# Places of VectorE sums and scalings, and paired final stores, in a fused attention and gated feed-forward kernel

## The chip, the cores and the metric

The kernel runs on one core of a Trainium2 chip. The metric is the device time of one execution in microseconds (us); for several executions the median is given. TensorE (PE) multiplies matrices into PSUM banks, VectorE (DVE) and ScalarE (ACT) work element by element, GpSimd (POOL) broadcasts rows, and SyncE (SP) issues the stores. Each engine takes its instructions in the order of the program and waits for the others by semaphores.

## The reference

Linear attention over 8 batches with 8 heads, 1024 tokens and 64 columns a head, then a feed-forward layer with a gate over the 8192 tokens:

```python
k_proj = np.einsum('ks,bhsd->bhkd', E, k)              # 64 rows instead of 1024
v_proj = np.einsum('ks,bhsd->bhkd', F, v)
attn = softmax(scale * q @ k_proj.T)                   # over the 64 rows
x = (attn @ v_proj) as 8192 tokens x 512
gate = 1 / (1 + exp(-(x @ w_gate)))                    # 512 x 1536
out = (gate * (x @ w_val)) @ w_out                     # 1536 x 512, float32
```

Inputs and output are float32; the kernel multiplies in bf16 and accumulates in float32.

## The kernel before, in words

**Tiles.** The tokens of a batch are worked in two blocks (`blk`) of 512. The attention of a batch leaves `xT`, 512 columns on four tiles of 128 partitions, for both its blocks. For a block, `x @ w_gate` is done whole (`g_step`, four matmuls of 512 columns), and `x @ w_val` and the product with `w_out` as Strassen-like products: seven half-size products in place of eight, for which VectorE first forms sums and differences of the operands. `xs_sums` (L1426) forms those of `x`, `s_sums` (L1228) those of the hidden values `hT`; `s_sums(blk, n, ms)` makes sum number n for the rows `ms`, where `A` = (0, 4) and `Z` = (4, 6) are two thirds and one third of them. Sum 1 writes S1, sum 2 S2 (from S1), sum 3 A21 in its place, sum 4 A12 in its place (from S2).

**Order.** The order on every engine is written out by hand. For the batches b = 1 to 7 a loop makes six units u, each a third of a block, with nine slots j: the pieces `p1`, `p26`, `p57`, `p4` of the value product (L1464, L1483 are their VectorE work: `hidden` and `v_add`), `g_step`s between them, and in slot 0 of the next unit the piece `p3` of the unit before. `on(u, j, fn)` puts other work behind slot j of unit u, in the order in which it was registered. `o0` = 2b - 1 and `o1` = 2b are the blocks whose product with `w_out` falls into this batch: `first_products` at (2, 0) and (5, 0), `last_products` at (2, 2) and (5, 2). `first_products(blk, hooks)` calls its hooks at fixed points; hook -1 lies between the product A12 x B21 and `add_snap(0, ...)`, which clears that product's bank, hook 0 behind `s_sums(blk, 4, ...)`, and hook 1 at the end.

**Attention in the background.** While batch b's feed-forward work runs, `attention(b + 1)` is laid between. At (3, 0) `outputs3` ends with eight small transfers (`gather`, L904) and 16 broadcasts on GpSimd (`spread`, L917), which give each of eight tiles its reciprocal denominators; `mul(r, g)` (L949) then scales that tile of `xu` into `xT`. There are eight scalings a batch. The last batch has no attention to prepare. Batch 0 has an order of its own, `todo` with `put(i, fn)`: there `bc2(R)` spreads the denominators of the second half by matmuls into two PSUM banks, and `scale` (L688) writes `xT` from them.

**Waits.** `Plan.add` notes what an instruction reads and writes, and waits are made of it. A matmul that starts a new product in a PSUM bank waits for whoever read that bank last, so `v_add`, `add_snap` and the gate (L1150) hold up TensorE if they are late:

```python
def p26():
    a = held_v["a"]
    held_v["c"] = c = FF.take()
    v_product(blk, q, c, "A12", "B21", start=True, stop=True)
    v_add(0, c)
    ...
def p57():
    a, c = held_v["a"], held_v["c"]
    v_product(blk, q, c, "S1", "T1", start=True)
```

**The end.** `final_products` (from L1330 on) does the last block's product with `w_out`, with VectorE's `plus` (L1347) and `add_snap` (L1280), and stores each quarter when it is there: eight stores of 128 rows of 1 KB from SP (L1340). The stores of the other blocks (L1325) have rows of 2 KB.

Of the kernel before, what the change touches and what calls it, by code (L numbers as in the profile page):

```python
# [118 lines left out]
def bass_linformer_attn__then__ffn_glu_sigmoid_kernel(  # L119
# [11 lines left out]
    B = q.shape[0]  # L131
# [6 lines left out]
    with contextlib.ExitStack() as es:  # L138
# [71 lines left out]
        ost = sbuf("ost", [P, 4, DM], FP32)  # L210
# [358 lines left out]
        def half_unit(hf, ring):  # L569
# [86 lines left out]
            def bc(R):  # L656
                bks = [ring.next(), ring.next()]
                for c in range(4):
                    for g in range(2):
                        n = 2 * R + g  # L660
                        nn = slice(32 * n, 32 * n + 32)
                        mm(
                            bks[g],
                            bank[bks[g]][:, c * P : (c + 1) * P],
                            (bsel8 if hf else bsel8f)[nn, c, :, :].rearrange("p h d -> p (h d)"),
                            (rhl if hf else rden)[nn, 0:P],
                            ["bsel8", ("rhl", R)] if hf else ["bsel8f", ("rden", 0, R)],
                            tp=(32 * n, 0),
                        )
                if hf:  # L670
                    for g in range(2):
                        scale(R, g, bank[bks[g]], xu[:, 2 * R + g, :], [("xu", 2 * R + g)], bks[g])

                def keep(g):
                    act(
                        xu[:, 2 * R + g, :],
                        bank[bks[g]][:, :],
                        [],
                        [("xu", 2 * R + g)],
                        b=bks[g],  # L680
                    )

                return keep
# [646 lines left out]
        def final_products(blk):  # L1330

            a, b, c, e0 = [AA.take() for _ in range(4)]
            e1 = FF.take()

            def store(tt, col, sem):
                t = 2 * (2 * (blk % 2) + tt % 2) + tt // 2
                cc = slice(256 * col, 256 * col + 256)
                add(
                    "SP",
                    lambda e: e.dma_start(out_v[blk // 2, t][:, cc], ost[:, tt, cc]),  # L1340
                    r=[("ost", tt, col)],
                    dma=sem,
                )

            def plus(o, keys, n, bk, jj):
                dve(
                    lambda e: e.scalar_tensor_tensor(  # L1347
                        o, bank[bk][:, jj], 0.5, snap[n][:, jj], ALU.mult, ALU.add
                    ),
                    [("snap", n)],  # L1350
                    keys,
                    b=bk,
                )

            product(blk, a, "A11", "B11", True)
            keep_snap(0, a)
            product(blk, c, "S1", "T1", True, True)
            product(blk, a, "S2", "T2")
            keep_snap(1, a)
            plus(snap[1], [("snap", 1)], 1, c, slice(0, 512))  # L1360
            product(blk, b, "A12", "B21", True, True)
            s_sums(blk, 4, (0, 6))
            add_snap(0, b, 0, 0)
            product(blk, a, "A21", "T3")
            keep_snap(2, a)
            add_snap(2, c, 1, 1)
            product(blk, e0, "A12", "B22", True, True, (0,))
            plus(ost[:, 0, 256:512], [("ost", 0, 1)], 1, e0, slice(0, 256))
            product(blk, a, "A22", "T4", stop=True)
            o, keys = quarter(1, 0)  # L1370
            act(o, bank[a][:, :].rearrange("p (j c) -> p j c", j=2), [], keys, b=a, scale=0.5)
            product(blk, e1, "A12", "B22", True, True, (1,))
            plus(ost[:, 1, 256:512], [("ost", 1, 1)], 1, e1, slice(256, 512))
            for tt, col in ((0, 0), (1, 0), (2, 1), (3, 1), (0, 1), (2, 0), (3, 0)):
                store(tt, col, f"out{tt}")
            store(1, 1, "outlast")

# [244 lines left out]
        put(5, lambda: (sc2(0), sc2(1)))  # L1624
        put(5, second_loads)
        put(7, lambda: (den2(), xo2(0), xo2(1)))
        put(9, lambda: (bc2(0), bc2(1)))
        for i, fn in zip((12, 14, 15, 16, 17, 18, 19, 19, 20, 21, 22), attention(1)):
            put(i, fn)
        put(16, lambda: (load_k(2), load_v(2), load_q(2)))  # L1630
# [27 lines left out]
        for b in range(1, B):  # L1658
            todo, at = [], {}
            for u in range(6):  # L1660
                K = 6 * b + u
                p1, p26, p57, p4, p3 = v_pieces(K)
                todo += [
                    last_piece,
                    p1,
                    lambda K=K: g_step(K, 1),
                    p26,
                    lambda K=K: g_step(K, 2),
                    p57,
                    lambda K=K: g_step(K, 3),  # L1670
                    p4,
                    (lambda K=K: g_step(K + 1, 0)) if K + 1 < 6 * B else (lambda: None),
                ]
                last_piece = p3

            def on(u, j, fn):
                put(9 * u + j, fn)

            def h_sums(blk, ms, *ns):
                return lambda: [s_sums(blk, n, ms) for n in ns]  # L1680

            def x_sums(blk, *ns):
                return lambda: [xs_sums(blk, n) for n in ns]

            A, Z = (0, 4), (4, 6)
            o0, o1 = 2 * b - 1, 2 * b
            if b == 1:
                first = {1: lambda: (vt_sums(1), vt_sums(4), x_sums(2, 1, 2, 3, 4)())}
                on(0, 0, lambda: first_products(o0, first))
                on(0, 2, lambda: last_products(o0))  # L1690
                on(0, 4, x_sums(3, 1, 2, 3, 4))
                on(2, 0, h_sums(o1, A, 1))
                on(2, 4, h_sums(o1, A, 2, 3))
            else:
                on(0, 4, h_sums(o0, A, 1, 2))
                on(1, 0, h_sums(o0, A, 3))
                on(1, 0, h_sums(o0, Z, 1))
                on(1, 4, h_sums(o0, Z, 2, 3))
                first = {
                    0: x_sums(o1 + 1, 1, 2, 3, 4),  # L1700
                    1: h_sums(o1, A, 1, 2, 3),
                }
                on(2, 0, lambda: first_products(o0, first))
                on(2, 2, lambda: last_products(o0))
            if b + 1 < B:
                n = attention(b + 1)
                late, keep_kv, mul = n["late"], n["keep_kv"], n["mul"]
                ks = 1 if b == 1 else 0
                for u, name in ((ks, "scores"), (ks + 1, "mixed")):
                    on(u, 0, n[name])  # L1710
                    on(u, 1, lambda: late("A0", 0))
                    on(u, 3, lambda: late("A0", 1))
                    on(u, 6, lambda: (late("A1", 0), late("A1", 1)))
                on(3, 0, n["outputs"])
                on(3, 0 if b + 2 < B else 4, h_sums(o1, Z, 1, 2, 3))
                on(3, 1, lambda: late("A0", 0))
                on(3, 3, lambda: late("A0", 1))
                on(3, 6, lambda: keep_kv(0))
                on(4, 1, lambda: keep_kv(1))
                on(4, 3, lambda: keep_kv(2))  # L1720

                on(4, 4, lambda: (mul(0, 0), mul(0, 1)))
                last = {
                    -1: lambda: mul(1, 0),
                    0: lambda: (mul(1, 1), mul(2, 0), mul(2, 1)),
                    1: lambda: (mul(3, 0), mul(3, 1)),
                }
                on(5, 0, lambda: first_products(o1, last))
                on(5, 4, x_sums(o1 + 2, 1, 2))
                on(5, 7, x_sums(o1 + 2, 3, 4))  # L1730
            else:
                on(3, 0, h_sums(o1, Z, 1, 2, 3))
                last = {1: h_sums(o1 + 1, A, 1, 2, 3)}
                on(5, 0, lambda: first_products(o1, last))
                on(5, 7, h_sums(o1 + 1, Z, 1, 2, 3))
            on(5, 2, lambda: last_products(o1))
            if b + 2 < B:
                kpd_ = [("kpD", R) for R in range(2)] if b == 1 else []
                load_at = (1, 4) if b == 1 else (0, 2)
                on(*load_at, lambda: (load_k(b + 2, kpd_), load_v(b + 2), load_q(b + 2)))  # L1740
                on(3, 4, transpose_q)
            for i, slot in enumerate(todo):
                slot()
                for fn in at.pop(i, ()):
                    fn()
            assert not at
# [31 lines left out]
```

## Time and profile before

| | |
|---|---|
| Median of 4 runs | 534.01 us (533.27 to 534.75) |
| Profiled execution: time, span | 533.24 us, 531.4 us |
| TensorE busy | 519.8 us, 98% of the span |
| VectorE busy | 407.4 us, 77% |
| ScalarE busy | 302.7 us, 57% |
| GpSimd busy | 133.5 us, 25% |
| Granted TensorE clock | 1.0 |

The span goes from the first to the last instruction of the profiled execution; the time of the same execution is 1.8 us longer. In the lists of groups and in the timeline, a line names start and busy time in us, then the engine, the line of the code, the operation, the tiles it writes and reads, their shapes, and how many instructions are merged; a bracket gives the idle time of the engine before it and what ended it. Many lines carry the number of a helper (L264 is every matmul, L268 every ACT instruction), so the tiles tell them apart: `wG` is the gate product, `wV` and `vT` the value product, `wO` and `wT` the product with `w_out`. In the waits, an engine stands left and what it waited for right, with the sum in us, the number of times and the longest. PEld is TensorE's loading of weights, which can run ahead of the matmuls.

### The profile page before, as it was taken

To read this page: it belongs to the slowest core of one execution; us is meant where nothing else is said; L and a number is where in the kernel's file an instruction comes from. 1 tells how busy PE (TensorE), PEld (TensorE's weight loads), DVE (VectorE), ACT (ScalarE), POOL (GpSimd) and SP (SyncE) were. 2 spreads that over 40 slices of the span, in tenths; PEclk is the share of its full clock that TensorE was granted. 3 is DMA by queue.
4 is the path that set the end of the run, shared out by engine and by line. 5 is a ranking of instruction groups with operands and counts; after the bars stand their busy time and mean duration, and the time that the engine had idled before them with its cause. 6 is when DMAs were issued, how large, how long until landed. Compare 5 with 4: busy or idle time off the path is not lost.

```text
span 531.4 us, 10382 instructions
## 1 busy us (share of the span) xinstructions
PE 519.8 (98%) x4137; PEld 347.4 (65%) x4137; DVE 407.4 (77%) x662; ACT 302.7 (57%) x544; POOL 133.5 (25%) x148
## 2 busy tenths in 40 slices
PE   5999999999999999999999999999999999999997
PEld 4544446656857667585766768576675867767676
DVE  4645495888987788877988789878888689887755
ACT  2554823687385564946567473755748464544541
POOL 9310200106700085002920048000740009200000
PEclk9999999999999999999999999999999999999999
DMA  9999999794293255911689233952520020202022
GB/s 171 200 199 203 161 203 214 151 177 87 35 228 63 80 92 85 230 42 47 88 165 153 80 60 36 220 96 80 92 80 1 1 83 2 81 0 80 1 81 79
DMA packets 77200, 56.18 MB, mean 106 GB/s; under 512 B 34848, under 2 KB 69344, under 8 KB 77152
## 3 DMA queue, kind: packets, MB, share of 16 engines
q0 software_dynamic: 33984, 29.89, 36.3%
q1 hardware_dynamic: 43168, 25.63, 19.8%
q8 instruction: 32, 0.52, 0.4%
q14 instruction: 16, 0.13, 0.1%
HBM read 60.29 MB, written 16.78 MB: 145 GB/s over the span
## 4 chain that ended last, share of the span: by engine, by line
PE 93%; DVE 3%; DMA 1%; issue 1%; POOL 1%; ACT 0%; SPq 0%; POOLq 0%; DVEq 0%
PE pF L264 60%; PE pA L264 32%; POOL KVs L917 1%; DMA EF<-in_F_dram 1%; DVE xT L949 1%; DVE rden L841 1%; DVE vsnap L1483 1%; DVE hT L1150 0%; DMA eT<-rden 0%; DVE rden L639 0%; DVE hS L1228 0%; DVE xT L688 0%; DVE ost L1280 0%; ACT vsnap L268 0%; ACT qT L268 0%
## 5 line engine op out<-in xcount | busy, mean ns | idle before, releaser
L264 PE MATMUL pF<-xT,wG 128*128 128x512 bf16 x768 | 197.9, 379 | 0.3
L917 POOL PARTITION_BROADCAST KVs<-eT x96 | 96.9, 1035 | 244.5 <-PE pF L264 191.7
L268 ACT ACTIVATE sig<-pF 128x512 f32<-128x512 f32 x192 | 115.6, 602 | 52.9 <-PE pF L264 50.9
L1483 DVE TENSOR_TENSOR vsnap<-pF,vsnap 128x512 f32<-128x512 f32 x126 | 86.8, 689 | 37.7 <-PE pF L264 28.0
L264 PEld LDWEIGHTS pF<-xT,wG 128*128 128x128 bf16 x768 | 73.7, 98 | 57.0 <-issue 1.7
L268 ACT ACTIVATE vsnap<-pF 128x512 f32<-128x512 f32 x126 | 75.3, 598 | 45.8 <-PE pF L264 43.1
L1464 DVE SCALAR_TENSOR_TENSOR hT<-sig,vsnap 128x512 bf16<-128x512 f32 x126 | 87.1, 691 | 6.2 <-ACT vsnap L268 0.5
L264 PE MATMUL pF<-xT,wV 128*128 128x256 bf16 (+1 forms) x432 | 76.1, 297 | 0.3 <-DVE hT L1150 0.3
L264 PE MATMUL pA<-wO,hT 128*128 128x256 bf16 x534 | 63.4, 273 | 0.0
L264 PEld LDWEIGHTS pF<-xT,wV 128*128 128x128 bf16 x432 | 40.6, 98 | 28.4 <-issue 5.3
L264 PEld LDWEIGHTS pA<-wO,hT 128*128 128x128 bf16 x534 | 52.2, 98 | 6.3
L264 PE MATMUL pF<-xS,wV 128*128 128x256 bf16 x336 | 50.5, 273 | 1.5 <-DVE vsnap L1483 1.4
L264 PE MATMUL pF<-xS,vT 128*128 128x256 bf16 x336 | 50.4, 273 | 0.0
L949 DVE TENSOR_TENSOR xT<-xu,KVs 128x512 bf16<-128x512 f32 x48 | 47.5, 1030 | 2.2 <-POOL KVs L917 1.7
L264 PEld LDWEIGHTS pF<-xS,wV 128*128 128x128 bf16 x336 | 32.0, 98 | 25.7 <-DVE vsnap L1483 6.6
L268 ACT ACTIVATE EF<-pA 128x512 f32<-128x512 f32 x30 | 17.9, 597 | 48.9 <-PE pA L264 48.9
L264 PE MATMUL pA<-wT,hT 128*128 128x256 bf16 x360 | 44.2, 273 | 0.0
L264 PE MATMUL pA<-wT,hS 128*128 128x256 bf16 x360 | 41.7, 273 | 0.0
L264 PEld LDWEIGHTS pA<-wT,hT 128*128 128x128 bf16 x360 | 35.1, 98 | 7.3 <-ACT snap L268 0.3
L264 PEld LDWEIGHTS pA<-wT,hS 128*128 128x128 bf16 x360 | 35.1, 98 | 4.2
L1280 DVE SCALAR_TENSOR_TENSOR ost<-pA,EF 128x512 f32<-128x512 f32 x29 | 20.0, 688 | 20.4 <-PE pA L264 20.4
L264 PEld LDWEIGHTS pF<-xS,vT 128*128 128x128 bf16 x336 | 32.9, 98 | 3.8
(112 smaller groups left out, 489.2 us busy)
## 6 DMA issues: line engine op xcount, KB each, us to landing
out_dram<-ost SPq DMA_DIRECT2D x57, 256.0 KB, 2.6
Qb<-in_q_dram POOLq DMA_DIRECT2D x7, 1024.0 KB, 20.2
KVs<-in_k_dram POOLq DMA_DIRECT2D x7, 1024.0 KB, 12.5
KVs<-in_v_dram POOLq DMA_DIRECT2D x7, 1024.0 KB, 16.6
wO<-in_moe_w_out_dram POOLq DMA_DIRECT2D x1, 1536.0 KB, 12.7
wG<-in_moe_w_gate_dram POOLq DMA_DIRECT2D x5, 256.0 KB, 17.5
wV<-in_moe_w_val_dram POOLq DMA_DIRECT2D x5, 256.0 KB, 18.0
KVs<-in_k_dram POOLq DMA_DIRECT2D x2, 512.0 KB, 7.6
```

What stands on the lines that cost most here:

```text
L264: return add("PE", lambda e: e.matmul(o, lhsT, rhs, **kw), r=r, x=[("bank", b)])
L268: return add("ACT", lambda e: e.activation(o, i, func, scale=scale), r=r, w=w, x=x)
L841: lambda e: e.reciprocal(rden[:, cc], bank[bk][:, cc]),
L917: lambda e, n=n, i=2 * rnd + c, j=j, parts=parts: e.partition_broadcast(rb[0:parts, n, :], rrow[32 * j : 32 * j + 1, i, :], channels=parts),
L949: lambda e: e.tensor_tensor(xT[s][:, r, :, 256 * g : 256 * g + 256], xu[:, n, :].rearrange("p (f c) -> p f c", f=2), y.rearrange("p (f c) ...
L1280: lambda e: e.scalar_tensor_tensor(o, bank[bk][:, :].rearrange("p (j c) -> p j c", j=2), 0.5, snap[n].rearrange("p (j c) -> p j c", j=2), ...
L1464: lambda e: e.scalar_tensor_tensor(o, sg[:, :, cc], 1.0, x.rearrange("p (j c) -> p j c", j=2), ALU.add, ALU.mult,),
L1483: lambda e: e.tensor_tensor(o, bank[bk][:, :], o, ALU.add),
```

## The change

It has five parts, and the arithmetic stays the same.

- In the last but one batch (b = 6), the scalings of the last batch's attention each come later: `mul(0, 0)` behind p4 at (4, 7) rather than both of `mul(0, *)` at (4, 4), three then two more at the hooks as before but each one further on, and `mul(3, 1)` at (5, 4).
- In the last batch (b = 7), the sums of block o0 are laid out otherwise: sum 1 of `A` stays at (0, 4); sum 2 of `A` and sum 1 of `Z` come at (1, 4), sum 2 of `Z` at (2, 0), and both sums 3 at hook -1 of `first_products`.
- In the last batch, the sums of `Z` of block o1 come at (3, 4) instead of (3, 0).
- In batch 0, the scalings of the second half are done two behind slot 9 and two behind slot 10, instead of four behind slot 9; the matmuls of `bc2` stay behind slot 9.
- In `final_products`, `add_snap(0, b, 0, 0)` comes ahead of `s_sums(blk, 4, ...)`, and the stores of two tiles with the same columns become one: five stores, three of them with 128 x 2 rows of 1 KB.

```diff
-                if hf:
+                def scales():
                     for g in range(2):
                         scale(R, g, bank[bks[g]], xu[:, 2 * R + g, :], [("xu", 2 * R + g)], bks[g])
+
+                if hf:
+                    return scales
...
-            def store(tt, col, sem):
-                t = 2 * (2 * (blk % 2) + tt % 2) + tt // 2
+            def store(tts, col, sem):
+                t = [2 * (2 * (blk % 2) + tt % 2) + tt // 2 for tt in tts]
                 cc = slice(256 * col, 256 * col + 256)
                 add(
                     "SP",
-                    lambda e: e.dma_start(out_v[blk // 2, t][:, cc], ost[:, tt, cc]),
-                    r=[("ost", tt, col)],
+                    lambda e: e.dma_start(
+                        out_v[blk // 2, t[0] : t[-1] + 1 : 2].rearrange("t p c -> p t c")[:, :, cc],
+                        ost[:, tts[0] : tts[-1] + 1, cc],
+                    ),
+                    r=[("ost", tt, col) for tt in tts],
                     dma=sem,
                 )
...
             product(blk, b, "A12", "B21", True, True)
+            add_snap(0, b, 0, 0)
             s_sums(blk, 4, (0, 6))
-            add_snap(0, b, 0, 0)
...
-            for tt, col in ((0, 0), (1, 0), (2, 1), (3, 1), (0, 1), (2, 0), (3, 0)):
-                store(tt, col, f"out{tt}")
-            store(1, 1, "outlast")
+            for tts, col in (((0, 1), 0), ((2, 3), 1), ((0,), 1), ((2, 3), 0)):
+                store(tts, col, f"out{tts[0]}")
+            store((1,), 1, "outlast")
...
-        put(9, lambda: (bc2(0), bc2(1)))
+        late = []
+
+        def spread2():
+            now = bc2(0)
+            late.append(bc2(1))
+            now()
+
+        put(9, spread2)
+        put(10, lambda: late[0]())
...
-                on(0, 4, h_sums(o0, A, 1, 2))
-                on(1, 0, h_sums(o0, A, 3))
-                on(1, 0, h_sums(o0, Z, 1))
-                on(1, 4, h_sums(o0, Z, 2, 3))
+                if b + 1 < B:
+                    on(0, 4, h_sums(o0, A, 1, 2))
+                    on(1, 0, h_sums(o0, A, 3))
+                    on(1, 0, h_sums(o0, Z, 1))
+                    on(1, 4, h_sums(o0, Z, 2, 3))
+                else:
+                    on(0, 4, h_sums(o0, A, 1))
+                    on(1, 4, h_sums(o0, A, 2))
+                    on(1, 4, h_sums(o0, Z, 1))
+                    on(2, 0, h_sums(o0, Z, 2))
...
+                if b + 1 == B:
+                    first[-1] = lambda: (h_sums(o0, A, 3)(), h_sums(o0, Z, 3)())
...
-                on(4, 4, lambda: (mul(0, 0), mul(0, 1)))
-                last = {
-                    -1: lambda: mul(1, 0),
-                    0: lambda: (mul(1, 1), mul(2, 0), mul(2, 1)),
-                    1: lambda: (mul(3, 0), mul(3, 1)),
-                }
+                if b + 2 < B:
+                    on(4, 4, lambda: (mul(0, 0), mul(0, 1)))
+                    last = {
+                        -1: lambda: mul(1, 0),
+                        0: lambda: (mul(1, 1), mul(2, 0), mul(2, 1)),
+                        1: lambda: (mul(3, 0), mul(3, 1)),
+                    }
+                else:
+                    on(4, 7, lambda: mul(0, 0))
+                    last = {
+                        -1: lambda: mul(0, 1),
+                        0: lambda: (mul(1, 0), mul(1, 1), mul(2, 0)),
+                        1: lambda: (mul(2, 1), mul(3, 0)),
+                    }
+                    on(5, 4, lambda: mul(3, 1))
...
-                on(3, 0, h_sums(o1, Z, 1, 2, 3))
+                on(3, 4, h_sums(o1, Z, 1, 2, 3))
```

## The prediction

> **What bounds the kernel now.** I read three views of the profile in this order: the busy times with the chain of waits, the waits of TensorE, and the timeline around each gap.
>
> ```profile
> PE 519.8 (98%) x4137; PEld 347.4 (65%) x4137; DVE 407.4 (77%) x662; ACT 302.7 (57%) x544; POOL 133.5 (25%) x148
> ...
> PE 93%; DVE 3%; DMA 1%; issue 1%; POOL 1%; ACT 0%; SPq 0%; POOLq 0%; DVEq 0%
> ```
>
> TensorE streams nearly all the time and makes up 93% of the chain. No matmul is removed here, so only the moments in which it stands still can be won, and the stores after its last product. VectorE is at 77%, yet it runs in program order: a sum put ahead of a short addition that TensorE is about to need makes TensorE wait.
>
> ```profile
> PE pF L264 <- DVE vsnap L1483: 1.4, 4, 0.8
> PE pF L264 <- DVE hT L1150: 0.3, 1, 0.3
> ```
>
> Only 1.7 us of plain waits stand on VectorE, too little to price a change by, since a weight load usually waits first. So I measured gaps in the timeline: the start of the next group, less the start of this one, less the pace seen where nothing waits (0.216 us for 512 columns, 0.109 for 256). Beside the repeated ones of 0.1 to 0.2 us, the gaps after the start are 0.47 at 46.62, 0.94 at 444.78, 0.43 at 470.89, 0.36 at 493.46 and 0.19 at 525.96. These are the places that the diff touches. The largest:
>
> ```profile
> 442.02 2.10 DVE L949 TENSOR_TENSOR xT<-xu,KVs 128x512 bf16<-128x512 f32 x2 [0.69 <-POOL KVs L917]
> ...
> 442.97 1.03 PE L264 MATMUL pF<-xT,wG 128*128 128x512 bf16 x4
> ...
> 444.04 0.68 DVE L1483 TENSOR_TENSOR vsnap<-pF,vsnap 128x512 f32<-128x512 f32 x1
> ...
> 444.78 0.61 PE L264 MATMUL pF<-xS,wV 128*128 128x256 bf16 x4 [0.78 <-DVE vsnap L1483]
> ```
>
> Two scalings (L949) stand ahead of the addition (L1483) that frees the bank for the next product; four wG matmuls end their pace at 442.97 + 0.87 = 443.84, and the product starts at 444.78.
>
> **What the Trainium skill says.** "SBUF — State Buffer", section "Who interferes with whom": a VectorE instruction with two SBUF inputs contends with a GpSimd instruction that reads SBUF. The trace agrees: L949 takes 1145 ns in the median while the broadcasts (L917) run, 693 and 684 ns after the last one. "VectorE: DVE Perf Modes", section "Mode 2×_1P": 16-bit operands give two results per cycle; here a sum over 128x1024 bf16 takes 0.68 us, as 128x512 in f32. "DMA: Bandwidth & Descriptors", section "Anatomy of one DMA": most of a transfer's fixed 2 us is the confirmation of the write, so it does not shrink with size; here the 128 KB stores land 1.76 to 1.95 us after issue.
>
> **Part 1: last but one batch (b = 6).** The first scalings move behind the piece p4. No instruction is added or dropped: eight scalings as before. Then the addition follows its copy (ACT, 441.87 + 0.60): 442.49 to 443.18, before the product at 443.84, and 0.94 goes. What is late next? VectorE runs on in steps of start to start read off the trace: 0.60 for a PSUM operation, 0.71 if it needs its predecessor's result, 1.07 for a scaling beside broadcasts. Hidden sum at 443.17 (its product's start 442.53 + 0.64, as at other such pieces), second one 443.77, scaling 444.4, addition 445.5, hidden sum 446.2, scaling 446.8 (hook -1), add_snap of first_products 447.9 to 448.6. TensorE, from 443.84, needs 0.44 for its product and 36 matmuls of 0.109 (3.93), and wants that bank at 448.21; in the kernel before it wanted it at 449.15 and had it at 449.08. So a new wait of 448.64 - 448.21 = 0.43 arises, because two scalings instead of one now stand between the copies and add_snap. The later scalings wait as before for the last broadcast (454.69); the last one goes past the next piece's first sums, pushing those from 457.4 (in the new time) to 458.1 and the next addition to about 459.0 against a need at 459.9. I charge 0.07 for the thin margin at the next but one piece (addition ready 463.4 to 463.5, wanted 463.45). Gain: 0.94 - 0.43 - 0.07 = 0.44. Bounds: 0 (the backlog grows by half a microsecond) and 0.94 (no new wait).
>
> **Part 2: last batch, sums of the block before.** At 469.21 and 469.81 two sums (0.68 and 0.42) stand ahead of an addition that was ready at 469.34 and began at 470.15.
>
> ```profile
> 469.21 0.68 DVE L1228 TENSOR_TENSOR hT<-hT 128x1024 bf16<-128x1024 bf16 x1
> ...
> 469.81 0.42 DVE L1228 TENSOR_TENSOR hS<-hT 128x512 bf16<-128x512 bf16 x1
> ...
> 470.15 0.69 DVE L1483 TENSOR_TENSOR vsnap<-pF,vsnap 128x512 f32<-128x512 f32 x1
> ...
> 470.89 0.61 PE L264 MATMUL pF<-xS,wV 128*128 128x256 bf16 x4 [0.28 <-DVE vsnap L1483]
> ```
>
> They are spread over later places. At (1,4) a sum of 0.68 and one of 0.42 follow the hidden sum (470.05) and end by 471.7, before the next addition's copy is ready (472.1). One of 0.42 stands at (2,0), ending at 475.9; two (0.60 + 0.42) stand at hook -1, 475.8 to 476.8, with add_snap's product ready at 476.86. All five lie beside matmuls, so 0.43 is won. If that cover were missing, add_snap could be late by 0.3 before TensorE notices.
>
> **Part 3: last batch, (3,0) to (3,4).** Three sums (start to start 0.45, 0.34, 0.34: 1.13) held an addition ready at 491.98 until 492.72. After the move they run from 493.3 to 494.5, and the next addition's copy is ready at 494.77. Won: 0.36.
>
> **Part 4: first batch.** Four scalings (L688) start at 43.49, 0.60 apart, then the gate (L1150) at 45.89; TensorE waits for the gate until 46.62. With two scalings behind the gate, VectorE idles from 44.77 until that gate's product is there (44.97 + 0.10 = 45.07), then runs gate and two scalings to 45.07 + 0.60 + 0.60 + 0.68 = 46.95. The first matmul that needs them stood at 47.07 and now starts at 47.01. The gap moves rather than closes: 0.06 won (bounds 0 and 0.47). Nothing else takes those two banks before slot 12.
>
> **Part 5: the end.**
>
> ```profile
> 524.07 0.96 DVE L1228 TENSOR_TENSOR hT<-hT,hS 128x1536 bf16<-128x1536 bf16 x1
> ...
> 525.96 1.49 PE L264 MATMUL pA<-wT,hT 128*128 128x256 bf16 x12
> ...
> 528.14 0.42 DVE L1347 SCALAR_TENSOR_TENSOR ost<-pF,EF 128x256 f32<-128x256 f32 x1 [1.18 <-PE pF L264]
> ```
>
> With add_snap (0.60) ahead of this sum, the sum ends at 525.62, and the product behind it starts at 525.67 instead of 525.11. The wait at 525.96 swallows a part: the twelve matmuls start at 525.67 + 0.66 = 526.33, 0.37 late, and the last `plus` ends at 528.93 instead of 528.56. Against that, SP issues five stores instead of eight.
>
> ```profile
> L1340 SPq DMA_DIRECT2D out_dram<-ost x8: 332/436/460, 525.7 to 529.1; - x8
> ...
> DMA to landing us min/median/max: 1.8/1.9/1.9
> ```
>
> Now the last store waits in SP's queue behind two others: ready at 528.56, issued at 529.06, landed at 530.93. Afterwards the pair is issued at 528.55 (act ends 0.37 later than 528.17) and the last one at 528.95. If the pair costs SP and the DMA engines what two stores take together (some 0.9), the data ends some 0.2 later; if rows stream at the busiest pace (340 rows of 1 KB per us), some 0.1 earlier. I take a loss of 0.03, bounds -0.1 and +0.3: the compute is later by what the queue saves. Paired stores of this form do not occur in the trace.
>
> **Sum:** 0.44 + 0.43 + 0.36 + 0.06 - 0.03 = 1.26 us. The profiled execution (span 531.4, time 533.24, so 1.8 outside the span) would come to 532.0; it lies 0.77 below the median 534.01 of the runs shown. I take the difference from the median: 534.01 - 1.26 = 532.75, so 532.8.
>
> **Rivals.** A, the wait returns in full (24%): the backlog of scalings at the last but one batch holds first_products for as long as was won (0.94). For it: the need at 448.21 has no slack. Against it: only one scaling more lies ahead. Without part 1, 0.82 stays: 533.2. B, the gaps simply close (14%): broadcasts slow VectorE less in the new order, and no new wait arises; 0.94 + 0.43 + 0.36 + 0.06 = 1.79: 532.2. C, slower (4%): the pair at the end drains badly. It is issued at 528.55; 256 KB stores land after 2.1 us at best, 2.6 in the median and 10.0 at worst, the last of the group at 515.22 after 4.3. From 1.26 + (530.93 - 528.55) = 3.6 us to landing on, the pair eats the whole gain; at 4.9 the end is 2.5 later: 535.3. Against it: the slow landings come behind backlogs that the last stores lack.
>
> **How the numbers follow.** A run of this kernel tells apart about 0.2%, that is 532.94 and 535.08. The forecast has 58%, of which some 46 lie below 532.94, since its terms are known to about 0.3. Faster: 0.46 + 0.14 = 0.60; same: 0.12 + 0.24 = 0.36; slower: 0.04. The range goes from 532.0 (B and some spread of the runs) to 533.6 (A and the worse bound of the end).
>
> **What would show it.** Right: no gap before the product after p4 at b = 6, but one of about 0.4 before the thirteenth matmul on hS in first_products; no gaps at 470 and 493; a gap of 0.4 before the first matmul on i = 2 in the first pair of block 1; at the end 0.5 before e0's six matmuls. Wrong: a paired store that lands after more than 3 us, or a gap at b = 6 that merely moved.

## The result, and the profile after

The changed kernel takes 533.53 us in the median of 31 runs, the kernel before 534.09 in 51 runs beside them; the ratio is 0.9986 with a 95% interval of 0.9981 to 0.9992. That is 0.4 to 1.0 us less time, or about 0.75. The forecast was 532.8, a gain of 1.26: the time lies within the range given (532.0 to 533.6), by 0.07 us, but the gain is 0.14% and not the 0.24% that was held likeliest. A second set gave 533.76 against 534.25 (ratio 0.9994, 0.9986 to 1.0002), which lies just outside that range.

The profiled execution of the changed kernel took 533.85 us with a span of 532.1, longer than the 531.4 shown of before. This says nothing on the change: its first product of the gate starts at 21.7 us instead of 20.25, because the first loads landed later. From there on it is shorter. Two lines of its page:

```profile
span 532.1 us, 10378 instructions
...
PE 93%; DVE 3%; DMA 2%; POOL 1%; issue 0%; ACT 0%; DVEq 0%; ACTq 0%; POOLq 0%
```

The chain is TensorE's as before; its DMA share is 2% instead of 1%, all of it a load of `v` that came late. To compare kernels I therefore take a distance inside one execution: from the first matmul on `wT`, at about 90 us, to the end of the span. It was 442.91 us before and is 442.14 after (442.14 again in a second profile of the same kernel); part 4, which lies ahead of that point, adds 0.03. The sum of 0.80 agrees with the ratio of the first set; in the second it lies at the edge of the interval.

The waits of TensorE after the change, with the waiting matmul left and what it waited for right:

```profile
PE pA L264 <- DVE ost L1283: 0.6, 1, 0.6
PE pA L264 <- DVE hT L1231: 0.4, 1, 0.4
...
PE pF L264 <- DVE xT L691: 0.3, 1, 0.3
...
PE pF L264 <- DVE vsnap L1489: 0.2, 1, 0.2
```

Of the four waits on `vsnap` (1.4 us) one is left, at 518.51. Three others on VectorE are new: on `add_snap` at b = 6 (L1283), on the sum in the end (L1231), and on the scalings of the first batch (L691).

**The last but one batch.** The timeline of the changed kernel, from the addition that was late before:

```profile
443.89 0.69 DVE L1489 TENSOR_TENSOR vsnap<-pF,vsnap 128x512 f32<-128x512 f32 x1 [1.17 <-ACT vsnap L268]
...
444.36 1.03 PE L264 MATMUL pF<-xT,wG 128*128 128x512 bf16 x4
444.56 0.69 DVE L1470 SCALAR_TENSOR_TENSOR hT<-sig,pF 128x512 bf16<-128x512 f32 x1
445.17 1.05 DVE L1470 SCALAR_TENSOR_TENSOR hT<-sig,vsnap 128x512 bf16<-128x512 f32 x1
445.23 0.60 PE L264 MATMUL pF<-xS,wV 128*128 128x256 bf16 x4
...
446.15 1.15 DVE L952 TENSOR_TENSOR xT<-xu,KVs 128x512 bf16<-128x512 f32 x1
...
448.54 1.15 DVE L952 TENSOR_TENSOR xT<-xu,KVs 128x512 bf16<-128x512 f32 x1
449.61 0.68 DVE L1283 SCALAR_TENSOR_TENSOR ost<-pA,EF 128x512 f32<-128x512 f32 x1
...
450.35 0.39 PE L264 MATMUL pA<-wT,hS 128*128 128x256 bf16 x2 [0.59 <-DVE ost L1283]
```

The product after p4 starts at 445.23, with no gap: 444.36 + 0.87. The thirteenth matmul on `hS` was wanted at 449.59 and starts at 450.35, a new gap of 0.76. The second hidden sum (`hidden`, L1470; the one with both inputs, `sig` and `vsnap`, in SBUF) is the line to look at: 1.05 us instead of 0.69.

**The last batch.** Both gaps are closed. At the first, in the changed kernel:

```profile
470.65 0.69 DVE L1489 TENSOR_TENSOR vsnap<-pF,vsnap 128x512 f32<-128x512 f32 x1 [0.39 <-PE pF L264]
470.82 1.03 PE L264 MATMUL pF<-xT,wG 128*128 128x512 bf16 x4
...
471.68 0.49 PE L264 MATMUL pF<-xS,wV 128*128 128x256 bf16 x3
```

VectorE now waits for the product (0.39 idle) and not the product for VectorE; 470.82 + 0.86 is the start of the next group.

**The first batch.** The gap stands two matmuls later than before, and is almost as long (0.45 against 0.47). The stretch from the matmuls on `vT` at 44.15 to the next ones on `EFT` takes 7.92 us in all eight traces with this part and 7.95 to 7.96 in all six without, so the part is worth 0.03:

```profile
46.51 0.69 DVE L1153 SCALAR_TENSOR_TENSOR hT<-sig,pF 128x512 bf16<-128x512 f32 x1 [0.30 <-PE pF L264]
...
47.11 1.28 DVE L691 TENSOR_TENSOR xT<-pA,xu 128x512 bf16<-128x512 f32 x2
...
48.45 0.39 PE L264 MATMUL pF<-xT,wG 128*128 128x512 bf16 x1 [0.29 <-DVE xT L691]
```

**The end.** The order on VectorE and what TensorE does with it, then the five stores:

```profile
524.50 0.69 DVE L1283 SCALAR_TENSOR_TENSOR ost<-pA,EF 128x512 f32<-128x512 f32 x1
525.11 0.95 DVE L1231 TENSOR_TENSOR hT<-hT,hS 128x1536 bf16<-128x1536 bf16 x1
...
526.11 0.83 PE L264 MATMUL pA<-wO,hT 128*128 128x256 bf16 x6 [0.44 <-DVE hT L1231]
...
526.78 1.47 PE L264 MATMUL pA<-wT,hT 128*128 128x256 bf16 x12
...
528.94 0.42 DVE L1353 SCALAR_TENSOR_TENSOR ost<-pF,EF 128x256 f32<-128x256 f32 x1 [1.47 <-PE pF L264]
```

```profile
L1343 SPq DMA_DIRECT2D out_dram<-ost x5: 372/394/467, 525.2 to 529.4; - x5
...
DMA to landing us min/median/max: 2.1/2.2/2.2
```

The six matmuls wait for the sum, 0.60 in all. A pair costs SP hardly more than a single store (0.37 to 0.39 us against 0.33 to 0.46), but each store lands 2.1 to 2.2 us after issue, against 1.8 to 1.9 before, the small last one too. From the end of the last `plus` to the end of the span it is now 2.69 us, before 2.86.

### The profile page after: what moved, and what is told of

Its sections match the earlier page's. It is cut to its first block, busy times and chain, and to the rows that moved or that the text cites. A ratio compares the mean times of both kernels' runs of the same rounds, so it can differ in the third digit from the quotient of the medians.

```text
span 532.1 us, 10378 instructions
## 1 busy us (share of the span) xinstructions
PE 519.7 (98%) x4137; PEld 347.6 (65%) x4137; DVE 407.9 (77%) x662; ACT 302.7 (57%) x544; POOL 133.6 (25%) x148
## 4 chain that ended last, share of the span: by engine, by line
PE 93%; DVE 3%; DMA 2%; POOL 1%; issue 0%; ACT 0%; DVEq 0%; ACTq 0%; POOLq 0%
PE pF L264 62%; PE pA L264 31%; DMA KVs<-in_v_dram 2%; DVE xT L952 1%; DVE hT L1153 0%; DVE rden L844 0%; POOL KVs L282 0%; POOL Qb L282 0%; DVE ost L1283 0%; DVE vsnap L1489 0%; DVE xT L691 0%; DVE rden L639 0%; DVE hT L1231 0%; DVE EF L1353 0%; ACT EF L268 0%
## 5 line engine op out<-in xcount | busy, mean ns | idle before, releaser
L1470 DVE SCALAR_TENSOR_TENSOR hT<-sig,vsnap 128x512 bf16<-128x512 f32 x126 | 87.3, 693 | 6.2 <-ACT vsnap L268 0.5
L1283 DVE SCALAR_TENSOR_TENSOR ost<-pA,EF 128x512 f32<-128x512 f32 x29 | 20.0, 689 | 19.3 <-PE pA L264 19.3
```

The lines of the kernel that those rows point to most:

```text
L1283: lambda e: e.scalar_tensor_tensor(o, bank[bk][:, :].rearrange("p (j c) -> p j c", j=2), 0.5, snap[n].rearrange("p (j c) -> p j c", j=2), ...
L1470: lambda e: e.scalar_tensor_tensor(o, sg[:, :, cc], 1.0, x.rearrange("p (j c) -> p j c", j=2), ALU.add, ALU.mult,),
```

## The experiments

Every kernel is set beside the kernel before in ratio and interval, where it was timed, and by the distance from the first matmul on `wT` to the end of the span of its profiled execution.

| kernel | ratio to before (95%) | distance, us | against before |
|---|---|---|---|
| before | | 442.91 | |
| changed | 0.9986 (0.9981 to 0.9992) | 442.14 | -0.77 |
| sums_only | 0.9990 (0.9978 to 1.0001) | 442.09 | -0.82 |
| p1_only | 1.0014 (0.9997 to 1.0032) | 442.92 | +0.01 |
| tail_only | 0.9998 (0.9984 to 1.0012) | 443.15 | +0.24 |
| tail_pairs | 0.9992 (0.9983 to 1.0001) | 442.72 | -0.19 |
| tail_swap | one run | 443.30 | +0.39 |
| after_gap | one run | 442.62 | -0.29 |
| after_hook | 0.9977 (0.9964 to 0.9991) | 441.94 | -0.97 |
| best | 0.9975 (0.9966 to 0.9984) | 441.55 | -1.36 |
| after_again | 0.9994 (0.9986 to 1.0002) | 442.14 | -0.77 |
| after_order | 0.9978 (0.9971 to 0.9986) | 441.73 | -1.18 |
| best_again | 0.9981 (0.9970 to 0.9993) | 441.53 | -1.38 |
| best_late | one run | 441.56 | -1.35 |

The two pairs of equal kernels differ by 0.00 and 0.02 us in the distance, far less than the intervals of the ratios, 0.3 to 1.0 us to each side. So the distances carry the verdicts on parts, and the ratios those on whole kernels.

My theory after the result: of 0.46 us missing, about 0.26 is a wait of VectorE for GpSimd's broadcasts at b = 6, and 0.2 is the end. The rivals: the parts do not add up, and the end is set by the data of the stores.

**Parts alone: sums_only, p1_only.** The kernel before with parts 2 and 3 of the change, and with part 1 (the diffs of those places as shown above).

> The kernel before with the moves of the last batch's sums alone (parts 2 and 3). Theory (gains are what the traces' matmul starts show, part by part): the gaps of 0.43 and 0.36 us at 471 and 493 close, nothing else moves, about 533.3 against 534.1, ratio 0.9985. Rival (the gain shows in the trace but is given back at the end, since the stores set the end): gaps close, but the time stays within 0.3 us of the kernel before.

> The kernel before with the moves of the scalings at b = 6 alone (part 1). Theory (a hidden sum with two SBUF inputs waits for a running broadcast too, which the prediction left out): the gap of 0.94 goes, one of about 0.75 comes ahead of the thirteenth matmul on hS, net -0.15 to -0.2 us. The prediction's own step: new gap 0.43, net -0.44. Rival A of the prediction: new gap 0.94, net 0.

The sums give -0.82, as the theory had it, and nothing is given back. The scalings alone give nothing (+0.01), where the theory had -0.15 to -0.2. The gap of 0.94 goes and one of 0.76 comes, as expected, but the 0.18 that is left is lost again in the last batch. In the kernel with the scalings alone:

```profile
473.12 0.42 DVE L1228 TENSOR_TENSOR hS<-hT 128x512 bf16<-128x512 bf16 x1
473.45 0.68 DVE L1483 TENSOR_TENSOR vsnap<-pF,vsnap 128x512 f32<-128x512 f32 x1
...
474.19 0.33 PEld L264 LDWEIGHTS pF<-xS,wV 128*128 128x128 bf16 x4 [0.91 <-DVE vsnap L1483]
474.19 0.61 PE L264 MATMUL pF<-xS,wV 128*128 128x256 bf16 x4 [0.41 <-DVE vsnap L1483]
```

The wait that was 0.28 at this place in the kernel before is 0.41, since TensorE comes earlier to it and VectorE's backlog is the same: counted from the first matmul on `wT`, the addition starts at 381.63 in both kernels, and the product behind it at 382.38, against 382.37 before. In the changed kernel the sums have left this place; the same product starts at 381.76, against 381.93 with the sums alone, so part 1 is worth about 0.18 there. This is why the distances of the parts, 0.01 - 0.82 + 0.24 = -0.57, fall short of the whole by 0.2. Rival A of the prediction was right in the sum for the part alone, though not in its gap of 0.94.

**What delays the second hidden sum: after_gap.** The broadcasts from the seventh on are told to come after that sum:

```diff
+                    spread(0, (0, 1, 2))
+            def rest():
+                keys = [("hT", 1, 8, 1), ("hT", 1, 9, 1)]
+                spread(0, (3,), keys)
+                spread(1)
...
+                    on(4, 7, n["rest"])
                     on(4, 7, lambda: mul(0, 0))
```

> The changed kernel, with the last ten of the 16 broadcasts of the last attention held back until the second hidden sum at (4, 7) is done, so that no broadcast runs beside that sum. Theory (the new gap of 0.76 at b = 6 is larger than predicted because that sum waited 0.37 us for a broadcast): the sum takes 0.69 us instead of 1.06 and the gap before the thirteenth matmul on hS shrinks to about 0.4; the later broadcasts end about 1 us later and may open a gap of up to 0.8 further on. Rival (the backlog comes from the scalings alone): the sum still takes about 1.05, or it takes 0.69 and the gap stays above 0.65.

```profile
444.79 0.69 DVE L1480 SCALAR_TENSOR_TENSOR hT<-sig,vsnap 128x512 bf16<-128x512 f32 x1
...
445.39 0.69 DVE L953 TENSOR_TENSOR xT<-xu,KVs 128x512 bf16<-128x512 f32 x1
445.56 3.57 POOL L920 PARTITION_BROADCAST KVs<-eT  x3 [1.02 <-DVE hT L1480]
...
447.90 2.78 PE L264 MATMUL pA<-wT,hS 128*128 128x256 bf16 x24
...
456.59 0.69 DVE L953 TENSOR_TENSOR xT<-xu,KVs 128x512 bf16<-128x512 f32 x1 [1.59 <-POOL KVs L920]
...
457.80 0.68 DVE L1499 TENSOR_TENSOR vsnap<-pF,vsnap 128x512 f32<-128x512 f32 x1
...
458.54 0.61 PE L264 MATMUL pF<-xS,wV 128*128 128x256 bf16 x4 [0.86 <-DVE vsnap L1499]
```

The sum takes 0.69 instead of 1.05, and so does the scaling behind it instead of 1.15, since it started before the next broadcast. All 24 matmuls on `hS` run on without a gap: the wait of 0.76 was made by broadcasts, more of it than I expected. The price appears where it was foreseen. A scaling waits for the last broadcast, which ends 0.7 us later than in the changed kernel (both counted from the first matmul on `wT`), and a gap of 1.0 opens behind it, where up to 0.8 was expected, and one of 0.20 further on. So this is a proof and not a remedy.

**One scaling fewer ahead of add_snap: after_hook.**

```diff
                     last = {
-                        -1: lambda: mul(0, 1),
-                        0: lambda: (mul(1, 0), mul(1, 1), mul(2, 0)),
-                        1: lambda: (mul(2, 1), mul(3, 0)),
+                        0: lambda: (mul(0, 1), mul(1, 0), mul(1, 1)),
+                        1: lambda: (mul(2, 0), mul(2, 1), mul(3, 0)),
                     }
```

> The changed kernel with mul(0, 1) taken from hook -1 to hook 0 of first_products at b = 6, and the later ones moved on by one inside the hooks. Theory: add_snap comes 1.07 us earlier, 0.3 before it is needed, the gap of 0.76 goes, and no other comes: 0.7 to 0.8 us below the changed kernel, about 1.4 below the kernel before (ratio 0.9973). Rival (the wait moves on again, to the bank of last_products or to the pieces after it): at most 0.3 below the changed kernel.

The theory failed here: the distance is 0.20 shorter than that of the changed kernel, not 0.75, and the rival holds. The gap of 0.76 is gone, but the wait moved on to the pieces after it, 0.38 and 0.19 us:

```profile
456.45 0.69 DVE L952 TENSOR_TENSOR xT<-xu,KVs 128x512 bf16<-128x512 f32 x1 [0.70 <-POOL KVs L920]
...
457.66 0.68 DVE L1489 TENSOR_TENSOR vsnap<-pF,vsnap 128x512 f32<-128x512 f32 x1
...
458.40 0.61 PE L264 MATMUL pF<-xS,wV 128*128 128x256 bf16 x4 [0.22 <-DVE vsnap L1489]
```

VectorE stands idle for 0.70 ahead of `mul(3, 0)`, which waits for the last broadcast, and the addition that TensorE needs stands behind it.

**That scaling later: best_late.** As best (below), with `mul(3, 0)` at (5, 3), behind that addition:

```diff
-                        1: lambda: (mul(2, 0), mul(2, 1), mul(3, 0)),
+                        1: lambda: (mul(2, 0), mul(2, 1)),
                     }
+                    on(5, 3, lambda: mul(3, 0))
                     on(5, 4, lambda: mul(3, 1))
```

> As the best version, with mul(3, 0) behind the next piece's additions at (5, 3). Theory (with one scaling fewer ahead of add_snap, the wait of 0.38 at the next but one piece comes from mul(3, 0), which waits for the last broadcast): that gap closes, and since VectorE has no time to spare a smaller one of 0.2 to 0.3 comes at the piece p3 behind it. Rival (VectorE's load alone makes the wait, not the broadcast): the gap before that product stays within 0.1 of 0.38.

```profile
456.73 0.59 PE L264 MATMUL pF<-xT,wG 128*128 128x512 bf16 x2
...
457.16 0.60 PE L264 MATMUL pF<-xS,wV 128*128 128x256 bf16 x4
...
459.75 0.68 DVE L1489 TENSOR_TENSOR vsnap<-pF,vsnap 128x512 f32<-128x512 f32 x1
...
460.49 0.61 PE L264 MATMUL pF<-xS,wV 128*128 128x256 bf16 x4
```

The gap at that product (457.16) closes, so the scaling ahead of the addition was its cause; the 0.70 us that it waits for the broadcast and the 0.6 of its own work are not told apart. A gap of 0.29 opens at the piece p3 that follows (460.49) and one of 0.30 further on. The sum stays: 0.58 against 0.56, and the distance with it (441.56 against 441.53). Between 442 and 465 us VectorE has no free time at the right places; shifting work within the stretch shifts the wait.

**The end in parts: tail_only, tail_pairs, tail_swap.** The kernel before with the changed end, with paired stores alone (the diff of `store` and its calls above), and with the changed order alone (`add_snap` ahead of `s_sums`).

> The kernel before with the changed end alone (part 5: add_snap ahead of the sum, and paired stores). Theory: the last plus ends 0.40 later, and the shorter queue saves only 0.17 from there to the end, so about +0.2 us. The prediction's own step: +0.03. Rival: pairs and order together are a gain of 0.2 or more.

> The kernel before with paired stores alone, the sum still ahead of add_snap. Theory: the last plus ends as before; the last store goes out at once instead of 0.5 us later and lands some 2.15 after issue instead of 1.88, so -0.2 to -0.3 us. Rival (the end is set by the store data, of which a pair has as much): no change, within 0.1 us.

> The kernel before with add_snap ahead of the sum alone, and eight single stores. Theory: the last plus ends 0.40 later; the early stores leave 0.9 earlier, but the last three still queue, so the last lands 0.4 later. Rival (the earlier start of the first stores clears the queue): the last store lands no later than before.

All three came as the theory had them, to 0.04 us: +0.24, -0.19 and +0.39. The order costs what it adds to the products, and the first stores' earlier start buys nothing back, since with single stores the last still goes out 0.47 us after the last `plus`. Pairs save that wait in SP's queue, and the longer landing takes back 0.27 of it. The line of the stores in the kernel with pairs alone shows landings as in the changed kernel:

```profile
L1340 SPq DMA_DIRECT2D out_dram<-ost x5: 372/394/465, 527.2 to 530.2; - x5
...
DMA to landing us min/median/max: 2.1/2.2/2.2
```

**Versions that beat both: after_order, best, best_again.** after_order is the changed kernel with the sum ahead of add_snap again; best is after_hook with that order too. after_again is the changed kernel beside them.

```diff
-            add_snap(0, b, 0, 0)
             s_sums(blk, 4, (0, 6))
+            add_snap(0, b, 0, 0)
```

> The changed kernel with the sum ahead of add_snap again in the end, paired stores kept. Theory (the changed order costs 0.4 us of products, and buys nothing since the last stores start at the last plus either way): 0.4 us below the changed kernel, ratio 0.9978 to the kernel before. Rival (the earlier first pair is needed, so that the later stores find the queue empty): no gain over the changed kernel.

> As the run with mul(0, 1) in hook 0, and the end with the paired stores but the sum ahead of add_snap again. Theory: both gains add up, another 0.4 to 0.5 us, about 1.9 below the kernel before (ratio 0.9964). Rival (the end is set by the store data): no more than 0.1 beyond the run with the hook alone.

> The changed kernel with mul(0, 1) in hook 0 and the sum ahead of add_snap, once more beside the others. Theory: 0.6 us below the changed kernel (0.4 of the end, 0.2 of the scalings), ratio 0.9974. Rival (the scalings give nothing): as the run with the order alone.

> The changed kernel once more, beside the other versions on one chip. All theories: 0.6 to 0.8 us below the kernel before.

Undoing the order gives 0.41 us of distance on the changed kernel, as expected, and 533.12 against 533.76 in the median, run side by side (ratios to before 0.9978 and 0.9994, with intervals that just touch). With the scaling moved as well, 0.2 more by the distance (441.53), as expected; by the time of the runs the two cannot be told apart (533.18). The 1.9 us below the kernel before that were expected of best did not come, since after_hook had fallen short: 1.4 by the distance. The changed kernel beside them was 0.5 below the kernel before in the median, less than the 0.6 to 0.8 expected. The version called best has medians of 533.01 and 533.18, below both kernels.

## Why the prediction was right or wrong

By the distances and gaps, in the prediction's own steps:

| step | forecast | measured |
|---|---|---|
| part 1, scalings at b = 6 | 0.44 (0.94 - 0.43 - 0.07) | 0.18 (0.95 - 0.75 - 0.02) |
| parts 2 and 3, sums of the last batch | 0.79 | 0.82 |
| part 4, first batch | 0.06 | 0.03 |
| part 5, the end | -0.03 | -0.24 |
| sum | 1.26 | 0.79 |

**Right** were the four places, the closing of both gaps in the last batch to within 0.03 us, the gap of the first batch that moves rather than closes, and the mechanism at b = 6: the wait returns at the thirteenth matmul on `hS`. That the time still fell into the range is in part luck: two terms were too good, by 0.26 and 0.21, and the time lies 0.07 inside the edge in the first set and 0.16 outside it in the second. The list of gaps in the prediction left out one of 0.32 at 98.43 and one of 0.28 at 518.11; the change touches neither, and both are still there after it.

**Wrong in size: part 1.** The failed step is "0.60 for a PSUM operation, 0.71 if it needs its predecessor's result, 1.07 for a scaling beside broadcasts". I gave the second hidden sum 0.60, though both its inputs lie in SBUF, as the scalings' do. It took 0.98 from start to start in the changed kernel. The section of the Trainium skill that I had named ("SBUF — State Buffer", "Who interferes with whom") says it of a VectorE instruction with two SBUF inputs in general, and that the order of issue decides which of the two engines waits; I applied it to the one kind that the profile's groups showed as slow. The trace of before had a sign, a hidden sum of 0.84 instead of 0.69:

```profile
445.24 0.84 DVE L1464 SCALAR_TENSOR_TENSOR hT<-sig,vsnap 128x512 bf16<-128x512 f32 x1
```

after_gap shows the cause: without a broadcast beside it the sum takes 0.69. The other steps of the chain were right: set to the same addition, the later instructions up to add_snap start 0.32 to 0.36 later than forecast, all from this sum on. The new wait is thus 0.32 larger than forecast; the charge for the later piece was 0.05 too high.

**Wrong in size: part 5.** The products came late as forecast (0.40 against 0.37). The failed step is the credit: "the compute is later by what the queue saves". SP's queue did save it: the last store left 0.04 us after the last `plus` instead of 0.49. But it then landed 2.15 us after issue instead of 1.88, so that only 0.17 of the 0.45 reached the end. The rows that the stores move show why (GB/s in 40 equal slices, first of 525.5 to 531.4 in the kernel before, then of 525.5 to 532 in the changed one):

```profile
GB/s 0 0 0 0 0 0 56 333 340 167 271 340 250 125 333 333 139 278 333 236 201 340 306 70 299 333 229 181 361 306 174 326 340 111 0 0 0 0 0 0
...
GB/s 0 0 0 38 302 353 347 347 221 6 0 0 0 0 0 252 347 347 353 328 353 334 107 0 0 0 25 271 347 359 353 334 328 328 76 0 0 0 0 0
```

With single stores the rate dips between them. In the changed kernel the last pair and the last store make one block without a dip, from 0.5 to 1.8 us after the end of the last `plus`: the small store waits for the pair's 256 rows, and the data has become the queue. The prediction's worse bound (some 0.2 later) has the right size for another reason: it supposed that a pair takes what two stores take together, some 0.9, and SP took 0.37 to 0.39. For rows at the busiest pace the prediction had 0.1 earlier; they came at about that pace, and the end was 0.24 later. tail_pairs and tail_swap separate the two: -0.19 and +0.39.

The gain of 0.44 hung on a chain with no slack, and the prediction said so of rival A. It still gave the forecast 58%, and most of that to a gain that a measurement can tell; with part 1 at 0.18 and part 5 at -0.24 the gain falls to 0.15% of the time.

What stays open: each part's distance is that of one execution, and no run has an order of the scalings at b = 6 that makes no new wait; after_hook and best_late shift it.

## What to carry to other kernels

Where an engine with a fixed order holds up another, count its work between two needs before moving a piece: a wait that is freed comes back at the next need if the stretch has no idle time, and in these runs only work taken out of the stretch (as the sums of the last batch) removed it. When costing VectorE beside GpSimd, look at the operands of every instruction, not at the group that is known to be slow. For a last store, add the rows that are queued ahead of it: fewer issues help only until the data is the queue (here 0.19 of 0.45 us).

## What the runs showed of the hardware

**A blocked instruction ends a fixed time after its blocker.** In the kernel before, 38 hidden sums and scalings took over 0.72 us beside a broadcast; every one ended 404 to 407 ns after the end of a broadcast that was running when it started (37 with 403 to 406 in the changed kernel). The inputs decide it: in each of the two traces 52 VectorE instructions of the same size, but with one input in PSUM, also started while a broadcast ran, and none took over 0.70. Hidden sums that started first kept their 0.69, and a broadcast then took longer: 1.24 us at 438.80 in the kernel before, against 0.79 for the shortest. So whether VectorE loses nothing or up to 0.46 depends on which comes first, by some tenths of a microsecond.

**The last store lands 0.40 to 0.41 us after its last row.** So it does in all 14 traces, whether it stands behind single stores or behind a pair; the rest of the 1.88 and 2.15 us from issue to landing lies ahead of that.

**The start scatters more than the change is worth.** Over the 14 profiled executions the first matmul on `wT`, ahead of which all kernels are alike but for the 0.03 us of part 4, lay between 88.5 and 91.8 us; the first load of `k` had landed between 8.1 and 10.2. In the one at 91.8 the granted clock had also been halved from 15.9 to 19.3 us; the other 13 lie between 88.5 and 90.2. The two executions of the best version have spans of 530.4 and 531.3 us with distances of 441.55 and 441.53, so the whole difference lies ahead of that matmul. This is why a profiled time alone can point the wrong way for a change of 0.1%; that the spread of all runs of a kernel (532.29 to 534.70 in the changed one) comes from the same place is likely, but not shown.
